# A linear-attention kernel with channel mix: whole 128-token chunks per head pair, casting loads with a DMA transpose, the max folded in by matmul, two-bank exponentials

One core of one Trainium2 chip. The metric is the device time of one execution in microseconds (us); lower is better. The kernel before takes 571.4 us (median of 4 runs in the comparison).

## The reference, cut to what matters

```python
def _attn_ref(q, k, v, w_phi):                       # 8 batches, 8 heads, 576 tokens, 64 wide; w_phi 64 x 128
    def phi(x):
        proj = np.einsum('bhsd,df->bhsf', x, w_phi)
        proj = proj - np.max(np.abs(proj), axis=-1, keepdims=True)
        return np.concatenate([np.exp(proj), np.exp(-proj)], axis=-1)
    q_p, k_p = (phi(q), phi(k))
    kv = np.einsum('bhsf,bhsd->bhfd', k_p, v)
    z = np.sum(k_p, axis=2)
    num = np.einsum('bhsf,bhfd->bhsd', q_p, kv)
    den = np.einsum('bhsf,bhf->bhs', q_p, z)[..., None] + 1e-06
    return num / den

def _moe_ref(x, mu_k, mu_r, w_k, w_v, w_r):          # x: 8 x 576 x 512, from the attention
    x_prev = # x one token later, zero first
    xk = mu_k * x + (1.0 - mu_k) * x_prev
    xr = mu_r * x + (1.0 - mu_r) * x_prev
    k = np.maximum(xk @ w_k, 0.0)                    # 512 -> 1024
    v = k * k @ w_v                                  # 1024 -> 512
    r = 1.0 / (1.0 + np.exp(-(xr @ w_r)))
    return r * v
```

The second part is called MoE below, as the code does, and its first three lines the mix. The work comes in 32 units, one for each pair of heads of a batch ("a pair"), four pairs a batch; after a batch's four pairs its mix and MoE follow, and these overlap with the next batch's pairs.

## The kernel before: the parts that the change touches

```python
def attention_pair(b, hp):
    for hh in range(2):                                   # 12 plain fp32 loads a pair, all from SP
        nc.sync.dma_start(out=q_nat[:, 0:NC4, 64*hh:64*hh+64], in_=q[b, h, 0:NC4*128, :]. ...)
        # ... q tail, k, k tail, v, v tail
    for (nat, T) in ((q_nat, qT), (k_nat, kT)):           # fp32 transposes on PE, evicted on DVE
        for ci in range(NC4):
            nc.tensor.matmul(ps_t[:, ci, :], lhsT=nat[:, ci, :], rhs=ident_f32, is_transpose=True, ...)
        # ... the tail chunk of 64 rows by itself
        nc.vector.tensor_copy(T[:, 0:NC4*128], ps_t...)
    # ... q and k projections, one bank at a time
    nc.vector.tensor_reduce(mk[:, 0:2, :], ps_pk, axis=AX.X, op=ALU.max, apply_absolute_value=True)
    nc.gpsimd.tensor_tensor(v1, vv, emki.to_broadcast(...), op=ALU.mult)     # exp(-max k) into v
    nc.gpsimd.tensor_tensor(v2, vv, emk.to_broadcast(...), op=ALU.mult)
    nc.scalar.activation(k_p[:, 0:2, :, :], ps_pk, AF.Exp)                   # 512 elements each
    # ...
    nc.scalar.activation(cq, mq, AF.Exp, scale=2.0)                          # max of q: a correction afterwards
    for hh in range(2):                                   # the heads one after the other
        # ... kv of this head (PSUM tag sm, one buffer), copy, nd1, nd2
        nc.vector.tensor_tensor(ndc, ps_nd2, cq..., op=ALU.mult)
        nc.vector.tensor_tensor(ndc, ndc, ps_nd1, op=ALU.add)
        nc.vector.reciprocal(rden, ndc[:, :, 64:65])
        nc.gpsimd.tensor_tensor(x_sc[...], ndc[:, :, 0:64], rden..., op=ALU.mult)
    # ... five transposes of x, copy to xT on ACT
```

## Time and profile before

| | before |
|---|---|
| time, median | 571.4 us (570.7 to 573.4, 4 runs) |
| span of the profiled run, mean granted TensorE clock | 571.3 us, 0.82 |
| busy: PE, DVE, ACT, POOL | 75%, 58%, 49%, 45% |
| pairs: first xT copy, mean distance, from the last one to the end | 37.3, 16.0, 37.7 us |
| DMA packets | 125,343 |

PE is the engine that multiplies matrices, DVE the vector engine, ACT the scalar engine, POOL is GpSimd, and SP issues DMAs. No engine is full. The reading that matters is the last line but one: 32 pairs follow each other at 16 us, so a pair's chain of waits sets the time, and what a change is worth shows in the distance between equal instructions of neighbouring pairs. The lines that carry this are in the prediction.

### The profile page before, as it was taken

The page shows a single profiled execution, that of the slowest core. Times are in us where ns is not written, and L with a number is a line of the kernel's source. Part 1 is how long each engine was busy: PE and PEld are TensorE (multiplying, and loading weights), DVE is VectorE, ACT ScalarE, POOL GpSimd, SP SyncE. Part 2 cuts the span into 40 slices and gives each one's busy share as a digit, 9 for nine tenths or more (in the row PEclk, how much of TensorE's full clock was granted, in tenths as well). Part 3 has the DMA queues.
Part 4 walks back from the last instruction along what each step waited for, and adds up shares of the span by engine and source line. Part 5 has one row for each costly group of instructions (what it writes and reads, how often), then busy time and mean ns, then how long its engine had stood idle before and what let it go on. Part 6 is the DMA issues. An engine that isn't in the chain of part 4 may idle for free. (4 is left out here: it accounts for less than half of the span.)

```text
span 571.3 us, 9500 instructions
## 1 busy us (share of the span) xinstructions
PE 428.0 (75%) x3200; PEld 259.8 (45%) x3200; DVE 330.9 (58%) x691; ACT 280.4 (49%) x780; POOL 255.7 (45%) x575
## 2 busy tenths in 40 slices
PE   0366655779787896779787896779787896779797
PEld 0144443555355443555355543555355444555352
DVE  0255458556865569556875469555775469555802
ACT  3553443565536544565436544565436553665141
POOL 2022334663346533663356433663256533663170
PEclk9995565789958897789968796789968796788979
DMA  7864222223322243223322233223312243001102
GB/s 198 251 151 106 64 57 47 63 63 100 89 46 53 61 126 73 63 62 98 87 46 64 61 118 71 64 63 89 99 39 56 63 117 84 0 2 38 46 1 83
DMA packets 125343, 43.68 MB, mean 76 GB/s; under 512 B 118512, under 2 KB 118640, under 8 KB 125296
## 3 DMA queue, kind: packets, MB, share of 16 engines
q1 hardware_dynamic: 125296, 43.09, 29.6%
q8 instruction: 25, 0.41, 0.3%
q14 instruction: 22, 0.18, 0.1%
HBM read 33.62 MB, written 9.44 MB: 75 GB/s over the span
## 5 line engine op out<-in xcount | busy, mean ns | idle before, releaser
L284 PE MATMUL ps_k<-xk,wk_bf 128*128 128x288 bf16 x512 | 115.4, 349 | 9.9 <-DVE xk L270 6.6
L288 POOL TENSOR_TENSOR kk<-krelu 128x288 bf16<-128x288 bf16 x128 | 86.4, 684 | 76.3 <-ACT krelu L287 67.8
L194 POOL TENSOR_TENSOR v<-v_nat,emk 128x650 bf16<-128x650 f32 x32 | 41.3, 1290 | 122.8 <-ACT emk L190 116.0
L251 POOL TENSOR_TENSOR x_sc<-ndc,rden 128x320 bf16<-128x320 f32 x64 | 49.9, 780 | 86.2 <-DVE rden L250 80.9
L287 ACT ACTIVATE krelu<-ps_k 128x288 bf16<-128x288 f32 x128 | 52.1, 417 | 67.0 <-PE ps_k L284 54.2
L302 PE MATMUL ps_v<-wv_bf,kk 128*128 128x512 bf16 x320 | 84.7, 381 | 0.0
L284 PEld LDWEIGHTS <-wk_bf 128*128 128x128 bf16 x512 | 56.9, 117 | 42.4 <-issue 25.5
L160 ACT ACTIVATE q_pT<-ps_pq 128x512 bf16<-128x512 f32 x64 | 38.6, 604 | 43.4 <-PE ps_pq L156 43.4
L246 DVE TENSOR_TENSOR ndc<-ps_nd,cq 128x325 f32<-128x325 f32 x64 | 31.9, 498 | 45.6 <-PE ps_nd L242 23.2
L228 PE MATMUL ps_kv<-v,k_p 128*128 128x65 bf16 x320 | 25.1, 222 | 40.7 <-POOL v L193 38.2
L228 PEld LDWEIGHTS <-k_p 128*128 128x128 bf16 x320 | 22.4, 114 | 72.4 <-issue 57.2
L134 DVE CAST qT<-ps_t 128x512 bf16<-128x512 f32 x32 | 22.1, 690 | 54.3 <-PE ps_t L129 54.3
L299 ACT ACTIVATE rt<-ps_r 128x512 bf16<-128x512 f32 x40 | 23.9, 597 | 55.9 <-PE ps_r L296 55.0
L296 PE MATMUL ps_r<-wr_bf,xr 128*128 128x512 bf16 x160 | 50.5, 412 | 0.0
L305 DVE SCALAR_TENSOR_TENSOR ob<-rt,ps_v 128x512 f32<-128x512 bf16 x40 | 27.3, 683 | 36.2 <-ACT xT L260 14.4
L234 DVE CAST kv_sb<-ps_kv 128x130 bf16<-128x130 f32 x64 | 18.8, 293 | 50.2 <-PE ps_kv L231 49.3
L161 ACT ACTIVATE q_pT<-ps_pq 128x64 bf16<-128x64 f32 x64 | 14.2, 222 | 66.6 <-PE ps_pq L157 66.6
L193 POOL TENSOR_TENSOR v<-v_nat,emki 128x650 bf16<-128x650 f32 x32 | 44.4, 1386 | 0.0
L302 PEld LDWEIGHTS <-kk 128*128 128x128 bf16 x320 | 29.3, 98 | 29.5 <-issue 9.4
L162 ACT ACTIVATE q_nT<-ps_pq 128x512 bf16<-128x512 f32 x64 | 38.4, 601 | 0.0
L238 PE MATMUL ps_nd<-kv_sb,q_pT 128*128 128x65 bf16 x320 | 25.8, 224 | 15.3 <-DVE kv_sb L234 15.3
L238 PEld LDWEIGHTS <-q_pT 128*128 128x128 bf16 x320 | 24.1, 120 | 27.5 <-issue 22.4
(81 smaller groups left out, 908.3 us busy)
## 6 DMA issues: line engine op xcount, KB each, us to landing
q_nat<-in_q_dram SPq DMA_DIRECT2D x64, 128.0 KB, 2.4
k_nat<-in_k_dram SPq DMA_DIRECT2D x64, 128.0 KB, 2.4
v_nat<-in_v_dram SPq DMA_DIRECT2D x64, 128.0 KB, 2.4
out_dram<-ob SPq DMA_DIRECT2D x32, 256.0 KB, 2.0
wstage<-in_moe_w_k_dram SPq DMA_DIRECT2D x1, 2048.0 KB, 8.3
wstage<-in_moe_w_v_dram SPq DMA_DIRECT2D x1, 2048.0 KB, 8.5
q_nat<-in_q_dram SPq DMA_DIRECT2D x64, 16.0 KB, 2.3
k_nat<-in_k_dram SPq DMA_DIRECT2D x64, 16.0 KB, 2.2
```

Of the source, the lines that this page charges most:

```text
L160: nc.scalar.activation(qp[:, 0:512], ps_pq, AF.Exp)
L162: nc.scalar.activation(qn[:, 0:512], ps_pq, AF.Exp, scale=-1.0)
L193: nc.gpsimd.tensor_tensor(v1, vv, emki.to_broadcast([128, NC, 2, 65]), op=ALU.mult)
L194: nc.gpsimd.tensor_tensor(v2, vv, emk.to_broadcast([128, NC, 2, 65]), op=ALU.mult)
L228: nc.tensor.matmul(ps_kv[:, 0:65], lhsT=k_p[:, ci, hh, :], rhs=v1[:, ci, hh, :], start=(ci == 0), stop=False)
L238: nc.tensor.matmul(ps_nd1[:, ci, :], lhsT=q_pT[hh][:, ci * 128:(ci + 1) * 128], rhs=kv_sb[:, 0:65], start=(ci == 0), stop=(ci == NC - 1))
L251: nc.gpsimd.tensor_tensor(x_sc[:, :, 64 * hh:64 * hh + 64], ndc[:, :, 0:64], rden.to_broadcast([128, NC, 64]), op=ALU.mult)
L284: nc.tensor.matmul(ps_k[:, 0:sw], lhsT=wk_bf[:, c, fc * 128:(fc + 1) * 128], rhs=xk[:, c, s0:s0 + sw], start=(c == 0), stop=(c == NDC - 1))
L287: nc.scalar.activation(krelu, ps_k[:, 0:sw], AF.Relu)
L288: nc.gpsimd.tensor_tensor(kk[:, fc, s0:s0 + sw], krelu, krelu, op=ALU.mult)
L296: nc.tensor.matmul(ps_r, lhsT=xr[:, c, cs:cs + 128], rhs=wr_bf[:, c, :], start=(c == 0), stop=(c == NDC - 1))
L302: nc.tensor.matmul(ps_v, lhsT=kk[:, fc, cs:cs + 128], rhs=wv_bf[:, fc, :], start=(fc == 0), stop=(fc == NFC - 1))
```

## The change

The intent: both heads of a pair go through one round instead of two, without a correction pass afterwards. Token p*4+j of a head stands in chunk j, row p, so that a load moves 1 KB a row; the 64-token tails of two heads share a chunk, which makes 9 full chunks. q and k are cast to bf16 by the load and transposed by one DMA per batch. The max of q is subtracted in PSUM: it is split into a high and a low bf16 part (`mhl`), transposed, and added to the projection by matmuls with a selector. Exponentials read two PSUM banks (1024 elements) at once. The tail rounds of two batches' MoE are joined.

Names used below: `v12` is v scaled by exp(-max k) and by exp(max k), in two POOL multiplies; `mT` is the transposed max of q, and the selectors are the matmuls that add it; `kv` is the product of k's exponentials with v12, `nd` holds numerator and denominator, `x_sc` is their quotient, and `xs` is its transpose, which the mix reads after a shift copy on POOL. The tails are the last 64 tokens of a head. A FIFO is an engine's queue, which it works off in order.

```diff
+            for (src, base) in ((k, 16), (q, 0)):
+                nc.gpsimd.dma_start(                                   # fp32 -> bf16
+                    out=flat[:, (base + 4 * a0) * 128:(base + 4 * a1) * 128]...,
+                    in_=src[b, hs, 0:SM, :].rearrange("h (p j) d -> p h (j d)", j=4))
+            # ... tails; v on SP
+            for (g0, g1) in rng:
+                nc.sync.dma_start_transpose(out=flatT[:, g0:g1, :], in_=flat[:, g0 * 128:g1 * 128])
...
+        ps_k = psum.tile([128, 8, 128], FP, name="ps_k", tag="P", bufs=2)       # two banks
+        ps_t = psum.tile([128, 4, 128], FP, name="ps_t", tag="B", bufs=2)       # tails; later mT
+        nc.vector.tensor_reduce(mk[:, :, 0:4], ps_k..., op=ALU.max, apply_absolute_value=True)
+        nc.vector.tensor_reduce(nm[:, 8:9], ps_t[:, 0, :], ..., negate=True)
+        nc.scalar.activation(em[:, 0, :], mkf, AF.Exp, scale=-1.0)
+        for pn in range(2):
+            nc.gpsimd.tensor_tensor(v12[:, pn, :, 0:64], vp..., em[:, pn, :]..., op=ALU.mult)
+        nc.scalar.activation(k_p, ps_k, AF.Exp)
+        nc.scalar.activation(k_n, ps_k, AF.Exp, scale=-1.0)
+        ps_q = psum.tile([128, 8, 128], FP, name="ps_q", tag="P", bufs=2)
+        nc.vector.tensor_reduce(nm[:, 0:8], ps_q, ..., negate=True)
+        nc.gpsimd.tensor_copy(mhl[:, 0:9], nm)
+        nc.gpsimd.tensor_tensor(mhl[:, 9:18], nm, mhl[:, 0:9], op=ALU.subtract)
+        nc.tensor.transpose(ps_mT, mhl, ident)
+        nc.vector.tensor_copy(mT, ps_mT)
+        ps_qT = psum.tile([128, 2, 4, 128], FP, name="ps_qT", tag="P", bufs=2)
+            nc.tensor.matmul(ps_qT[:, par, :, :]..., lhsT=wph[:, par, :], rhs=qkT[...], start=True, stop=False)
+                nc.tensor.matmul(ps_qT[:, par, g, :], lhsT=sel[:, 2 * g + par, :], rhs=mT, ...)
+        # t_p, t_n, q_p, q_n; kv (tag B) of both heads; kv copy; nd in two halves (tag B):
+            nc.vector.reciprocal(rden, ps_nd[:, :, 64])
+            nc.vector.tensor_tensor(x_sc[...], ps_nd[:, :, 0:64], rden..., op=ALU.mult)
+        # ps_x (tag B), copies to xs on DVE
...
     for b in range(B):
+        if b + 1 < B:
+            cur = load(b + 1, [(0, NP)])
         for hp in range(NP):
             attention_pair(...)
         if b >= 1:
             moe_batch(b - 1)
```

## The prediction

> **What bounds the kernel now.** I read the busy shares first, then the stretch before any MoE work (54 to 72 us) in order of time, then one tile's line for the pace.
>
> ```profile
> span 571.3 us, 9500 instructions
> PE 428.0 (75%) x3200; PEld 259.8 (45%) x3200; DVE 330.9 (58%) x691; ACT 280.4 (49%) x780; POOL 255.7 (45%) x575
> ```
>
> No engine is full. So the order of work, not an engine, sets the pace. The timeline from one k transpose's eviction to the next pair's shows it:
>
> ```profile
> 53.80 0.69 DVE L134 CAST kT<-ps_t 128x512 bf16<-128x512 f32 x1 [0.16 <-PE ps_t L129]
> ...
> 54.55 0.61 PE L175 MATMUL ps_pk<-wph,kT 128*128 128x256 bf16 x2
> ...
> 55.20 0.69 DVE L184 TENSOR_REDUCE mk<-ps_pk 128x4 f32<-128x512 f32 x1 [0.37 <-PE ps_pk L175]
> ...
> 56.99 0.21 ACT L191 ACTIVATE emki<-mk 128x10 f32<-128x10 f32 x1
> ...
> 57.18 1.27 POOL L194 TENSOR_TENSOR v<-v_nat,emk 128x650 bf16<-128x650 f32 x1 [5.56 <-ACT emk L190]
> ...
> 58.42 1.27 POOL L193 TENSOR_TENSOR v<-v_nat,emki 128x650 bf16<-128x650 f32 x1
> ...
> 59.74 0.43 PE L228 MATMUL ps_kv<-v,k_p 128*128 128x65 bf16 x5 [1.68 <-POOL v L193]
> ...
> 62.02 0.43 PE L228 MATMUL ps_kv<-v,k_p 128*128 128x65 bf16 x5 [0.43 <-ACT q_nT L163]
> ...
> 63.93 0.50 DVE L246 TENSOR_TENSOR ndc<-ps_nd,cq 128x325 f32<-128x325 f32 x1 [0.77 <-PE ps_nd L242]
> ...
> 65.58 0.72 POOL L251 TENSOR_TENSOR x_sc<-ndc,rden 128x320 bf16<-128x320 f32 x1 [1.62 <-DMA v_nat<-in_v_dram]
> ...
> 66.36 0.72 PE L256 MATMUL ps_x<-ident_bf,x_sc 128*128 128x128 bf16 x5
> ...
> 67.73 1.06 PE L129 MATMUL ps_t<-ident_f,k_nat 128*128 128x128 f32 x4
> ...
> 68.82 0.69 DVE L134 CAST kT<-ps_t 128x512 bf16<-128x512 f32 x1 [0.16 <-PE ps_t L129]
> ```
>
> The columns are start and duration in us. One head pair follows the next with hardly any overlap: 68.82 - 53.80 = 15.02 us. Two POOL multiplies, two kv/nd rounds in turn (one PSUM buffer, tag sm, passes from kv to the q tail and back), the POOL scaling, the x transposes and only then the next q/k transposes. Later, with MoE matmuls in the gaps, the big q projection of a first head comes at 301.18 and again at 315.54: 14.36 us. The MoE rides along for nothing.
>
> ```profile
> L258 ACT COPY xT<-ps_x x32: 585/587/590, 37.3 to 533.6; 128x512 bf16<-128x512 bf16 x32
> ```
>
> The xT copy ends each pair: (533.6 - 37.3)/31 = 16.0 us a pair on average, 37.3 us to the first, and 571.3 - 533.6 = 37.7 us for the last batch's MoE alone. This is the sum that I predict with: 37.3 + 31 x 16.0 + 37.7 = 571.
>
> **What the Trainium skill says.** (1) "ScalarE: Activation LUTs", What ACT_TABLE_LOAD costs: an activation with immediate scale takes 186 ns + 0.833 ns an element, and neighbours overlap by 93 ns. The trace agrees: 512 elements 604 ns (612 by it), 256 elements 393 to 406 (399). So 1024 elements in one instruction should take 1.04 us, against 2 x 0.60. (2) "DMA: Bandwidth & Descriptors", SWDGE vs HWDGE vs iDMA: a DMA that casts must be issued from GpSimd, whose cores write its descriptors; a transpose must come from SP or ACT. Before has neither (all loads are on SP's queue, 0.4 to 0.6 us of issue each), so no line shows what such an issue costs POOL. (3) "Advanced Engine Details and Errata", X-Bar Transpose (TRN2): 350 to 400 GB/s. A batch is 36 x 128 x 128 x 2 B = 1.18 MB, so 3.4 us, an estimate from that page; no run shows it yet. (4) "SBUF — State Buffer", Who interferes with whom: a DVE instruction with two SBUF inputs blocks against a POOL one that reads SBUF. It agrees: the xk mixes take 779 ns at least, 812 in the middle, up to 1478 beside POOL.
>
> **The change part by part, per pair unless said.**
>
> Transposes and loads. Gone: 10 fp32 transposes on PE, four evictions on DVE (2 x 0.69 + 2 x 0.22 = 1.8 us), six of the POOL memsets. In their place per batch 6 casting loads, 3 v loads and one DMA transpose, issued a whole batch ahead (two buffers), about 45 us before use. Bandwidth was 76 GB/s of the core and packets grow from 256 B to 1 KB, so they should hide.
>
> ACT. k and q exponentials: 4 x 1.04, tails 2 x 0.40, small 2 x 0.23: 5.4 us against 8.1 before (the xT copies of 0.81 move to DVE). With MoE (8 x 0.60 + 4.5 x 0.60, half of a tail round 1.1, over 4 pairs = 2.2): 7.6.
>
> DVE. Reduces of 1024 from PSUM at 1.07 ns an element (692 against 418 ns for 512 and 256): 2 x 1.24; tails 0.42 + 0.28; mT 0.22; kv 0.40; two of rden and multiply 2 x (0.18 + 0.48); xs copies 0.69 + 2 x 0.2. Sum 6.2, against 8.3. The cq correction (two passes over 325 a head) is gone. MoE: diff 1.4, mixes 8 x 0.73 + 8 x 0.15, outputs 4.5 x 0.68 = 11.5 a batch, 2.9 a pair. Together 9.1.
>
> POOL. v12 2 x 1.3, small ones about 0.5, squares (8 x 1.09 + 4 x 0.39)/4 = 2.6: 5.7, against 8. To this comes descriptor writing, for which I take 1 to 3 us an instruction: 1.5 to 4.5 a pair.
>
> PE, in columns: projections 9 x 256, max transpose 128, transposed q 2 x 512 + 8 x 128 + 2 x 128, kv and nd 1300 each, x 640: 7,976, against 8,232 (and the fp32 transposes took double). MoE, tails of two batches joined: 46,080 a batch against 49,152; 11,520 a pair. At 0.42 ns a column (four 512-column ps_r in 0.86 us at full clock): 8.2 us, at the granted 0.83: 9.9.
>
> So every engine fits in 10 us; now the chain. It runs through tag B (two buffers, five tiles a pair: ps_t, kv, nd, nd, x): the next ps_t needs the buffer of the last nd. From that release: ps_t 0.35, tail reduces 0.7, mhl on POOL 0.25, transpose 0.25, mT 0.25, selector matmuls and projection 1.0, exponentials 0.8 + 2.1 (beside them em 0.35 and v12 2.9 end at 4.2, before kv can start), last kv 0.4 (part hidden), kv copy 0.4, nd 0.8, rden and multiply twice 1.4. Sum 8.7. The k projection, its reduce and exponentials, and the q reduce (4.5 us of work) can be done in the pair before, as tag P frees in time. One round of kv/nd replaces two, and the POOL scaling and transposes have left the chain.
>
> DVE, PE and this chain are now close (9.1, 8.2 to 9.9, 8.7), so they collide: eight chain steps each find on DVE, ACT or POOL an instruction of 0.6 to 1.2 us under way about half of the time, 0.3 us each, 2.4. That gives **11.2 us a pair**.
>
> Start. 33 GpSimd DMAs (24 for the split first batch, 3 weights, 6 for the next) stand before the first v12 on POOL; at 1 us each, then some 9 us to the pair's end: 43 us. End: 6% fewer columns, but a tail round after: 38. Sum: 43 + 31 x 11.2 + 38 = **428 us**; I say 430.
>
> **Rivals.** (a) POOL becomes the bound: the big loads have 1024 rows each; if writing their descriptors takes 5 to 10 us, POOL is held some 25 us a batch, its FIFO stops v12 and the squares, and the start grows to 60 us or more: 13 us a pair, 470 to 510. For it: nothing measured; against it: POOL has the most slack. (b) The DMA transpose is slow, over the 45 us that the prefetch allows: then load, transpose and buffer release set the batch, 55 to 60 us: 500 to 560. Against it is the page's rate. (c) The chain overlaps worse than I think, since the scheduler puts v12 in front of mhl on POOL (adds 2.6 us) or queues the 1 us exponentials badly: 13.5 us a pair, 500. For it: before shows that orders once fixed are kept even where they idle (5.56 us on POOL). (d) All goes well, 9.7 us a pair, PE bound at nearly full clock: 380.
>
> **Range and chances.** Main line 430; (d) sets the low end at 385, (a) and (c) the high end at 500. Only (b) in its worst form, or a start and a POOL both far worse, reaches 560: 0.04 for slower, 0.04 for the same, 0.92 for faster.
>
> **What would show it.** The ps_x transposes should come every 11 us (right) or 13 and more (a or c). POOL idle before v12 waiting for em is the main line; POOL held by DMA issues is (a); PE waiting for a DMA of qkT after the first batch is (b); the mhl copies behind v12 are (c). ACT's busy time should fall to some 215 us, DVE's to 265, 1024-element exponentials to 1.04 us. DVE busy above 80% with PE's clock near 1 would mean an engine, not the chain, is the bound. The prediction falls if the first pair ends after 60 us or the pace is over 13.

## The result, and the profile after

| | before | after |
|---|---|---|
| time, median (range, 4 runs each) | 571.4 us (570.7 to 573.4) | 508.1 us (506.5 to 512.2) |
| ratio, 95% interval | | 0.889 (0.885 to 0.894) |
| granted TensorE clock of the profiled run | 0.82 | 0.94 |
| packets | 125,343 | 84,515 |

Every ratio here is from the fast runs of both kernels in the same rounds, so it is not quite the ratio of the medians quoted. The direction was right; 508 us is outside the range of 385 to 500.

First the busy line of the page, then the xs copies, which end each pair as the xT copies did before, and the kv copies, which I use as the beat below.

```profile
span 507.3 us, 7519 instructions
PE 336.2 (66%) x2832; PEld 194.5 (38%) x2832; DVE 296.2 (58%) x615; ACT 213.2 (42%) x389; POOL 247.1 (49%) x374
L267 DVE COPY xs<-ps_x x32: 409/418/425, 57.8 to 471.3; 128x512 bf16<-128x512 bf16 x32
L236 DVE CAST kv<-ps_kv x32: 413/429/430, 53.0 to 468.3; 128x260 bf16<-128x260 f32 x32
```

The sum that was predicted as 43 + 31 x 11.2 + 38 reads 57.8 + 31 x 13.34 + 36.0 = 507.3. The end is right; the start is 15 us too long and the pace, (471.3 - 57.8) / 31, costs 31 x 2.14 = 66 us. By place in the batch (batches 2 to 8), the mean distances of the kv copies are 15.9, 15.1, 11.3 and 9.9 us. The first pairs are the slow ones, and the last ones come close to the 8.7 us of the predicted chain. No engine is full: the busy shares of PE and ACT fell, DVE's stayed at 58%, and POOL's rose from 45% to 49%.

What PE waits for in front of the kv matmuls (group, with idle time and releasers last):

```profile
L231 PE MATMUL ps_kv<-v,k_p 128*128 128x65 bf16 x256 | 16.4, 209 | 58.4 <-POOL v L181 55.9 <-POOL mhl L197 2.5
```

55.9 us go to waiting for v12 on POOL. And the start, POOL in order of time:

```profile
32.72 0.20 POOL L197 CAST mhl<-nm 128x9 bf16<-128x9 f32 x1
44.87 0.93 POOL L118 DMA_DIRECT2D nat<-in_k_dram  x1 [11.95 <-DMA qkT<-nat]
45.82 2.49 POOL L178 TENSOR_TENSOR v<-vt,em 128x640 bf16<-128x640 f32 x2
48.25 0.27 POOL L181 CAST v<-em 128x20 bf16<-128x20 f32 x1
48.40 0.20 POOL L198 TENSOR_TENSOR mhl<-nm,mhl 128x9 bf16<-128x9 f32 x1
```

The issue of a load (0.93 us) stands in front of pair one's v12 and between the two steps of its max. It is the first load of the third batch, which cannot start before the first batch's DMA transposes free a nat buffer, so everything behind it on POOL stands still for 11.95 us. The same happens again at 62.55 us in front of the second pair.

### The profile page after: what moved, and what is told of

The parts are those of the page before. It is cut to its first block, busy times and chain, and to the rows that moved or that the text cites. A ratio compares the mean times of both kernels' runs of the same rounds, so it can differ in the third digit from the quotient of the medians.

```text
span 507.3 us, 7519 instructions
## 1 busy us (share of the span) xinstructions
PE 336.2 (66%) x2832; PEld 194.5 (38%) x2832; DVE 296.2 (58%) x615; ACT 213.2 (42%) x389; POOL 247.1 (49%) x374
## 2 busy tenths in 40 slices
DMA packets 84515, 40.92 MB, mean 81 GB/s; under 512 B 53120, under 2 KB 79360, under 8 KB 84480
## 4 chain that ended last, share of the span: by engine, by line
PE 31%; POOL 30%; DVE 18%; DMA 10%; issue 7%; ACT 4%; POOLq 0%; DVEq 0%; ACTq 0%
POOL v L178 15%; PE ps_v L319 6%; POOL kk L308 6%; DMA nat<-in_q_dram 5%; PE ps_h L304 5%; DMA qkT<-nat 4%; PE ps_kv L231 4%; PE ps_r L313 3%; DVE xr L290 3%; PE ps_nd L249 3%; DVE mk L161 2%; PE ps_k L153 2%; DVE tr L293 2%; POOL nat L124 2%; DVE x_sc L260 2%
## 5 line engine op out<-in xcount | busy, mean ns | idle before, releaser
L308 POOL TENSOR_TENSOR kk<-krelu 128x512 bf16<-128x512 bf16 (+1 forms) x96 | 85.1, 904 | 90.7 <-ACT krelu L307 90.2
L178 POOL TENSOR_TENSOR v<-vt,em 128x640 bf16<-128x640 f32 x64 | 82.6, 1314 | 1.1
L304 PE MATMUL ps_h<-xk,wk_bf 128*128 128x512 bf16 x256 | 77.2, 420 | 6.6 <-DVE xk L290 4.9
L307 ACT ACTIVATE krelu<-ps_h 128x512 bf16<-128x512 f32 (+1 forms) x96 | 46.2, 497 | 70.8 <-PE ps_h L304 61.6
L223 ACT ACTIVATE q_p<-ps_qT 128x1024 bf16<-128x1024 f32 x32 | 32.8, 1026 | 97.1 <-PE ps_qT L212 97.0
L185 ACT ACTIVATE k_p<-ps_k 128x1024 bf16<-128x1024 f32 x32 | 32.8, 1024 | 66.7 <-DVE mk L161 66.7
L231 PE MATMUL ps_kv<-v,k_p 128*128 128x65 bf16 x256 | 16.4, 209 | 58.4 <-POOL v L181 55.9
L161 DVE TENSOR_REDUCE mk<-ps_k 128x8 f32<-128x1024 f32 x32 | 39.1, 1221 | 24.6 <-PE ps_k L153 24.4
L194 DVE TENSOR_REDUCE nm<-ps_q 128x8 f32<-128x1024 f32 x32 | 39.0, 1218 | 14.2 <-PE ps_q L191 14.1
L207 PE MATMUL ps_qT<-qkT,wph 128*128 128x512 bf16 x64 | 29.3, 458 | 11.2 <-DVE nm L194 10.4
L319 PEld LDWEIGHTS <-kk 128*128 128x128 bf16 x288 | 26.4, 98 | 25.1 <-POOL kk L308 2.6
L290 DVE SCALAR_TENSOR_TENSOR xr<-diff,mu_r_t,xs 128x512 bf16<-128x512 bf16 x32 | 34.8, 1088 | 0.0
L224 ACT ACTIVATE q_n<-ps_qT 128x1024 bf16<-128x1024 f32 x32 | 33.4, 1044 | 0.0
```

What stands on the lines that cost most here:

```text
L161: nc.vector.tensor_reduce(mk[:, :, 0:4], ps_k.rearrange("p (h j) f -> p h j f", h=2), axis=AX.X, op=ALU.max, apply_absolute_value=True)
L178: nc.gpsimd.tensor_tensor(v12[:, pn, :, 0:64], vp.rearrange("p (s d) -> p s d", d=D), em[:, pn, :].to_broadcast([128, 10, D]), op=ALU.mult)
L194: nc.vector.tensor_reduce(nm[:, 0:8], ps_q, axis=AX.X, op=ALU.max, apply_absolute_value=True, negate=True)
L224: nc.scalar.activation(q_n, qT8, AF.Exp, scale=-1.0)
L231: nc.tensor.matmul(ps_kv[:, pn, h, :], lhsT=kx[:, c, :], rhs=v12[:, pn, 5 * h + j, :], start=(pn == 0 and c == 0), stop=False)
L290: nc.vector.scalar_tensor_tensor(out=xo[:, c, :], in0=diff[:, c, 0:SM], scalar=mu[:, c:c + 1], in1=xs[:, c, 0:512], op0=ALU.mult, op1=ALU.add)
```

## The experiments

18 kernels ran. All were compared with the kernel before on the same chip (its medians were 571.5 to 573.0 us). Where a result is wrong on purpose, the text says so; those five (e5, e6, e7, e9, e10) ran twice each, the others four or five times. An instruction's place in its engine's queue is fixed when the kernel is compiled: the compile-time scheduler takes the program's order as priority and its own simulated times. `tc.issue_after(x)` puts what stands in its block behind x on the same engine (in e1's trace no v12 multiply precedes the max subtraction any more; in the changed kernel's, 10 do).

### First four: was it the order on POOL, the loads, or the mix?

e1: v12 behind the max subtraction on POOL.

```diff
-        # emt and v12 multiplies ahead of the k exponentials
+        sub = nc.gpsimd.tensor_tensor(mhl[:, 9:18], nm, mhl[:, 0:9], op=ALU.subtract)
+        with tc.issue_after(sub.ins):
+            # emt and v12 multiplies
```

> The two v12 multiplies are queued on POOL behind the max subtraction of the same pair; nothing else changes. POOL-order theory: in 10 of 32 pairs of the changed kernel the multiplies (2.5 us) stand in front of the max copies, so the selector matmuls and the q exponentials wait 2.7 to 3.5 us longer; taking this away gives 25 to 35 us: about 478 us (470 to 490), and no pair with the subtraction after the multiplies. DVE-burst theory (the mixing of a batch in one go holds the slow pairs): within 1% of 508, because those pairs wait for DVE in any case.

Measured: 510.0 us (ratio 0.893), no gain. The first pairs of a batch still take 16.9 us. The issues of loads were left where they were, and POOL's wait for transposes in front of them rose from 25.0 to 30.4 us.

e2: the next batch's loads and the weights behind the first pair's v12.

```diff
             attention_pair(b, hp, qkT, vt)
+            if hp == 0:
+                with tc.issue_after(last_v12[0].ins):
+                    if b + 1 < B: cur = load(b + 1, [(0, NP)])
+                    if b == 0: load_weights()
```

> The loads of the next batch (and the weights) are queued on POOL behind the first pair's v12 instead of in front of it. Head-of-line theory: the first v12 starts near 27 us instead of 45.8, the first pair ends near 40 instead of 58 us, the second loses no 8 us either, and the whole gains 20 to 30 us: about 482 us. Rival (the DMA engines are full in the first 60 us, so the first batch's transposes and loads set the start in any case): first pair at 50 or later, gain under 8 us.

Measured: 488.3 us (0.853). The first kv copy comes at 30.9 us in place of 53.0, but the second one follows only 25.1 us later. DVE shows why:

```profile
41.06 0.22 DVE L203 COPY mT<-ps_t 128x128 bf16<-128x128 bf16 x1 [1.40 <-PE ps_t L201]
54.85 1.23 DVE L104 TENSOR_SCALAR wv_bf<-wv_bf 128x4096 bf16<-128x4096 bf16 x1 [13.56 <-DMA wv_bf<-in_moe_w_v_dram]
55.99 0.42 DVE L237 CAST kv<-ps_kv 128x260 bf16<-128x260 f32 x1
```

The halving of wv, which nobody needs yet, waits on DVE for its load, in front of the kv copy. The steady pace stays at 12.9 us over batches 2 to 8. So the gain is the start.

e3: the mix of each head pair right behind it instead of in one burst, with the shift copy of xs on POOL for each pair.

```diff
-    xk, xr = mix(b)                      # in one burst, after the next batch's pairs
+    attention_pair(b, hp, qkT, vt)
+    mix_pair(b, hp)                      # channel chunk hp only: shift copy (POOL), diff, xk, xr (DVE)
```

> The mixing of a batch's four column blocks (on DVE, about 13 us in one go after the batch) is done block by block right behind each head pair. DVE-burst theory: the first two pairs of a batch (16.6 and 14.2 us now, the last two 11.3 and 10.0) come down to about 12.5 each, and the time by 20 to 35 us: about 480 us; the last batch's end also shrinks by some 5 us. POOL-order theory: the first pairs stay slow because of the multiplies in front of the max copies and the loads; the gain is only the 5 us at the end, 500 us or more.

Measured: 592.2 us (1.036), much slower. POOL spent 200.9 us blocked on the shift copy that waits for the xs copy, in front of the next pair's v12. e4 was all three together:

> All three together. If the three losses are separate and the chain of 8.7 us plus collisions is the bound that is left, then 40 to the first pair, 31 x 11, and 33 at the end: about 415 to 435 us. If they are one loss seen from three sides, it stays near the best of the three single ones, 475 us or more.

Measured: 529.6 us (0.925). The shift copy's cost outweighs the rest. None of these shortened the pace by more than 0.2 us a pair (e3 and e4 raised it to 16.0 and 14.6), so my theory that GpSimd's queue or the mix burst sets it had no support left. It is not refuted for the mix: e3 spread the mix but added the waits on POOL, so it is no clean test.

### Four ablations: is it the MoE at all?

e5 leaves out mix and MoE between the pairs; e6 keeps the mix alone; e7 keeps the MoE alone, fed from fixed tiles; e8 is e1 and e2 together.

```diff
-        if b >= 1:
-            moe_batch(b - 1)
+        # e5: nothing      e6: mix(b - 1)      e7: moe_batch(b - 1) with xk, xr = fixed tiles
```

> The changed kernel without any mix or MoE work between the pairs (only the last batch's at the end, its rows stored for every batch: wrong result on purpose). Read from it: the intervals of the xs copies. Theory COLLISION (the pace is 13.3 us where the chain alone is 8.7 because the previous batch's mix and MoE stand in front of chain steps in the FIFOs): from batch 1 on every pair takes 8.5 to 10 us, the first of a batch too, 290 to 310 us from the first to the last xs copy. Rival BOUNDARY (attention itself is slow at a batch's start: loads on POOL that wait for transposes, buffers of nat/qkT): first pairs stay at 14 us or more, later ones at 9 to 10. Rival CHAIN (my chain was too short): all pairs stay over 11 us.

> As the run without MoE, but with the mix of the previous batch (GpSimd's shift copy, the DVE passes) in its place in the loop; MoE still only at the end (wrong result on purpose). Theory COLLISION by DVE: the mix is 11.5 us of DVE and a shift copy per batch, so the first two pairs of a batch gain 3 to 6 us together over the run without it; the mean pace rises by 1 to 2 us a pair. If the mix is not what hurts, it rises by under 0.5 us.

> The changed kernel with the MoE of each batch in place but fed from fixed tiles, no mix and no shift copy in the loop (wrong result on purpose). If PE/ACT/POOL work of the MoE is what collides: pace 12 us or more. If it is the mix: pace 9.5 to 10.5 us, 60 us or more off the time of the whole kernel.

> Both the v12 multiplies behind the max subtraction (alone without gain) and the loads of the next batch behind the first pair's v12 (alone 488 us). Theory ORDER ON POOL in its corrected form (both hold up the same chain step of the first pair, and taking away one lets the other take its place): 465 to 480 us, first pairs of a batch 14 to 16 us in place of 18. Rival (the order on POOL is worth nothing in steady state; what the second gained was the start alone): 484 to 495 us.

| | time | mean distance of kv copies, batches 2 to 8 | clock |
|---|---|---|---|
| after | 508.1 | 13.1 | 0.94 |
| e5, no mix, no MoE | 546.4 | 13.9 (14.1 to 14.6 nearly everywhere) | 0.63 |
| e6, mix alone | 514.4 | 12.6 | 0.68 |
| e7, MoE alone | 434.7 | 11.7 | 0.94 |
| e8, e1 and e2 | 490.2 | 13.0 | 0.89 |

The collision theory falls: take all the MoE away and the pairs get longer, not shorter. The attention alone runs at 14.3 us a pair in every batch (the whole kernel's first batch, which has no MoE beside it, shows the same 14.1 and 14.3). With work beside them the pairs come out in other orders and are shorter: the later pair's q reduce, read below, stands in front of the mT copy in 29 of 32 pairs of e5, but in 17 of e6, 19 of e7 and 14 of the changed kernel. The test is not clean, then: taking work away also changed the order, and the clock. e7 lies between its two forecasts: with the MoE in place, leaving out the mix takes 13.1 to 11.7 us. (e7's time has no end of its own, as its MoE does not wait for the last pairs; its distances are what to compare.) e8 adds nothing to e2.

So the steady pair of e5 had to be read step by step. From one x_sc to the next pair's q projection:

```profile
306.10 0.49 DVE L260 TENSOR_TENSOR x_sc<-ps_nd,rden 128x320 bf16<-128x320 f32 x1
...
307.30 1.23 DVE L161 TENSOR_REDUCE mk<-ps_k 128x8 f32<-128x1024 f32 x1 [0.60 <-PE ps_k L153]
308.44 0.48 DVE L260 TENSOR_TENSOR x_sc<-ps_nd,rden 128x320 bf16<-128x320 f32 x1
...
309.27 0.42 PE L158 MATMUL ps_t<-wph,qkT 128*128 128x256 bf16 x1
...
309.51 0.42 DVE L267 COPY xs<-ps_x 128x512 bf16<-128x512 bf16 x1 [0.59 <-PE ps_x L265]
...
310.61 0.28 DVE L166 TENSOR_REDUCE nm<-ps_t 128x1 f32<-128x128 f32 x1
...
311.49 2.48 POOL L178 TENSOR_TENSOR v<-vt,em 128x640 bf16<-128x640 f32 x2
...
311.67 1.23 DVE L194 TENSOR_REDUCE nm<-ps_q 128x8 f32<-128x1024 f32 x1 [0.78 <-PE ps_q L191]
312.81 0.21 DVE L202 COPY mT<-ps_t 128x128 bf16<-128x128 bf16 x1
...
314.23 0.60 PE L231 MATMUL ps_kv<-v,k_p 128*128 128x65 bf16 x8 [2.35 <-POOL v L181]
...
314.63 0.62 PE L207 MATMUL ps_qT<-qkT,wph 128*128 128x512 bf16 x1
```

Five delays can be counted; the granted clock of this stretch is 0.50. A later pair's k reduce (1.23) stands between the two x_sc multiplies. The xs copies (0.42 and two small ones) stand in front of the tail reduces, about 0.6. A later pair's q reduce stands in front of the mT copy: the transpose ended at 311.88, so 0.93. The kv matmuls that wait for v12 stand on PE in front of the selector group, which could have begun at 313.0: 1.6. And PE at this clock takes 2.0 us for projection and selectors, where a pair of the changed kernel at full clock took 1.2 (297.68 to 298.84 us). Together 5.2 us, of which 4.4 are places in the queues and 0.8 is the clock, and 14.3 - 5.2 = 9.1.

### Four: the order forced

e9 forces two places, e10 two more, both without MoE. e11 is e10's order in the whole kernel, e12 adds e2's loads.

```diff
+        with tc.issue_after(last_sel.ins):        # kv matmuls behind the selectors (PE)
             nc.tensor.matmul(ps_kv[...], ...)
+        with behind(last_mT):                     # k reduce (e9: and q reduce) behind the mT of the pair before (DVE)
             nc.vector.tensor_reduce(mk[:, :, 0:4], ps_k...)
+        with behind(last_xsc):                    # e10: q reduce behind the second x_sc of the pair before
             nc.vector.tensor_reduce(nm[:, 0:8], ps_q...)
+        with tc.issue_after(tail.ins):            # e10: xs copies behind the next pair's tail reduces
             nc.vector.tensor_copy(xs[...], ps_x...)
```

> The run without MoE took 14.3 us a pair in every batch, so MoE work is not what makes pairs long. New theory ORDER: FIFO places that the compile-time scheduler chose put work of the next pair, or work that waits for v12, in front of this pair's chain. Read from its steady pair: kv matmuls that wait for v12 stand on PE in front of the selector matmuls (1.2 to 1.6 us), the next pair's q reduce stands on DVE in front of the mT copy (1.0), its k reduce between the two x_sc multiplies (1.2), the xs copies in front of the tail reduces (0.8). Here two places are forced: kv behind the selectors on PE, and k and q reduces of a pair behind the mT copy of the pair before on DVE (wrong result on purpose, as before). ORDER: 14.3 falls by 2.2 to 12.0 us (11.5 to 12.6). Rival CLOCK (PE at half clock when idle, that is what makes the chain long): stays over 13.5.

> In addition the q reduce is forced behind the second x_sc of the pair before, and the xs copies behind the next pair's tail reduces. ORDER: another 1.2 + 0.8 less some 0.5 that the q reduce still costs the tail reduces: 10.5 us a pair (10 to 11). CLOCK: over 13 us.

> The same forced order in the whole changed kernel with MoE (correct result). ORDER: pairs three and four of a batch stay at 9.5 to 10.5 us, the first two fall from 17 and 14 to some 14 and 12 as mix work still stands between chain steps; 465 to 485 us in place of 508. If the pairs of the whole kernel are long for another reason (mix, loads), 500 to 515 us.

> The forced order and the next batch's loads and the weights behind the first pair's v12 (which alone made 488). If the two add up: 445 to 465 us. If the order gains nothing in the whole kernel: 484 to 492.

Measured without MoE: e5 546.4, e9 466.5, e10 414.0 us; a steady pair 14.3, 11.2 to 12.1, and 8.3 to 9.3. The clock was 0.63, 0.67 and 0.79: it rose as the waits went, so the 0.8 us of low clock went in part with them (in the stretch below it is 1.00 at the selectors and 0.50 from kv on). One pair in four of e10 in batches two to five, the one beside the loads, still takes 14.2 to 14.6: at 185 us POOL shows five issues of loads (the first after 4.07 us of waiting for a transpose) in front of its first max step, and a sixth and both v12 multiplies between the two steps. The same stretch of e10:

```profile
216.33 0.49 DVE L277 TENSOR_TENSOR x_sc<-ps_nd,rden 128x320 bf16<-128x320 f32 x1
216.74 1.21 DVE L210 TENSOR_REDUCE nm<-ps_q 128x8 f32<-128x1024 f32 x1
...
217.19 0.27 PE L168 MATMUL ps_t<-wph,qkT 128*128 128x256 bf16 x1
...
218.20 0.28 DVE L177 TENSOR_REDUCE nm<-ps_t 128x1 f32<-128x128 f32 x1
...
219.44 0.22 DVE L218 COPY mT<-ps_t 128x128 bf16<-128x128 bf16 x1 [0.34 <-PE ps_t L216]
...
219.72 0.82 PE L228 MATMUL ps_qT<-mT,sel 128*128 128x128 bf16 x8 [0.32 <-DVE mT L218]
...
221.81 0.60 PE L248 MATMUL ps_kv<-v,k_p 128*128 128x65 bf16 x8 [1.16 <-POOL v L196]
...
225.28 0.49 DVE L277 TENSOR_TENSOR x_sc<-ps_nd,rden 128x320 bf16<-128x320 f32 x1
```

225.28 - 216.33 = 8.95 us, close to the chain of 8.7 us of the prediction: all that still stands in front of a chain step is the q reduce, some 0.4 us, ahead of the tail reduces. The selectors follow mT at once, and kv waits for v12 behind them, beside the exponentials.

In the whole kernel e11 took 486.2 us (0.851): 22 us gained, 11 of them in the first batch. Over batches 2 to 8 the places read 17.5, 12.4, 10.8 and 9.6 (50.3 us a batch; after 52.2). With mix and MoE back, then, the forced order runs at 12.6 us a pair, where without them (e10) it ran at 9.7 over the same batches. e12 took 490.5: the two do not add up. In e12 the fourth pair comes 15 us earlier than in e11, though the second again comes 24 us after the first, held by the halving of wv; but the later batches run at 13.3 us a pair in place of 12.6.

### The last six: what holds the first pairs in the whole kernel

e13: e11 with the two max steps on DVE (the xs copies now stand behind the second of them). e14: the mix also held behind the first pair's mT. e15: also loads and weights behind the first v12, and the halving behind the fourth pair.

```diff
-        nc.gpsimd.tensor_copy(mhl[:, 0:9], nm)
-        nc.gpsimd.tensor_tensor(mhl[:, 9:18], nm, mhl[:, 0:9], op=ALU.subtract)
+        nc.vector.tensor_copy(mhl[:, 0:9], nm)                                   # e13
+        nc.vector.tensor_tensor(mhl[:, 9:18], nm, mhl[:, 0:9], op=ALU.subtract)
+        with tc.issue_after(first_mT[b + 1].ins): xk, xr = mix(b)                # e14
+        # e15: load(), load_weights() as in e2; the halving behind the fourth pair's mT
```

> The forced order, and the two small max subtraction steps on VectorE in place of GpSimd, which takes GpSimd out of the max chain (correct result). If GpSimd's queue is what holds the first pairs of a batch (v12, squares and load issues in front of the subtraction, 3 to 5 us): first pairs fall from 16 to 19 us to 13 or 14, the start by some 10 us, as pair one's and two's subtraction no longer waits behind blocked loads (though v12 still does, so perhaps not): 445 to 465 us. If not: 480 to 490.

> In addition the mix of the batch before is held on VectorE behind the first pair's mT copy (correct result). If the mix, which waits for GpSimd's shift copy, in front of mT is what holds the first pair: another 2 to 4 us a batch, 15 to 30 us less than the run before. If it is not: within 5 us of it.

> In addition the loads of the next batch and the weights behind the first pair's v12, and the halving of wv behind the fourth pair's mT copy (correct result). In the earlier runs with loads behind, the second pair came 24 us after the first, as the halving stood on VectorE waiting for its load (13.6 us idle) in front of the kv copy. Expected: first xs copy at 35 us, second 10 to 14 us later; 25 to 35 us less than the run before, 400 to 425 us. If the start is bound by the DMA instead (full for the first 62 us), the four first pairs still end at 85 to 95 us and it gains under 10.

Measured: 479.4, 477.2 and 465.5 us (0.837, 0.833, 0.812). The max on DVE is worth some 7 us; the first pairs stay at 17.7 us, so POOL's part in the max chain is not what holds them. Holding the mix gains nothing that the intervals separate. In e15 the fourth pair's kv copy comes at 64.3 us in place of 89.0 (e14), but only 11.6 us reach the end: the later batches got slower, 12.9 against 12.4 us a pair, so the 400 to 425 us were missed. Why is not tested. The loads' issues now stand behind the first v12 and in front of POOL's shift copy, for which the mix waits. And 28 of the 64 max steps on DVE took 0.42 to 1.23 us where the others took 0.17 to 0.26, each ending within 0.04 us of the end of a POOL instruction; over batches 2 to 8 they cost 25.4 us more than 0.18 us each would, 12.1 in e14 (13 such steps). That difference is as large as the slowdown, 28 x 0.5 us. PE in e15 at the border of two batches:

```profile
267.84 0.22 PE L274 MATMUL ps_nd<-kv,t_n 128*128 128x130 bf16 x1
...
269.94 1.89 PE L341 MATMUL ps_v<-wv_bf,kk 128*128 128x512 bf16 x8
271.67 1.03 PE L335 MATMUL ps_r<-wr_bf,xr 128*128 128x512 bf16 x4
272.66 1.89 PE L341 MATMUL ps_v<-wv_bf,kk 128*128 128x512 bf16 x8
...
274.61 0.60 PE L164 MATMUL ps_k<-wph,qkT 128*128 128x256 bf16 x4
```

The last nd of a batch ends at 268, and the next batch's first k projection comes at 274.6, behind a block of MoE matmuls: in the program, `moe_batch(b - 1)` comes before the next batch's pairs and so has priority. e16 moves the MoE of a batch behind the first pair of the batch after next; e17 spreads it in blocks of four between the pairs and takes the mix behind the first pair; e18 is e16's move in the changed kernel with no other edit.

```diff
             attention_pair(b, hp, qkT, vt)
+            if hp == 0 and b >= 2:
+                moe_batch(b - 2)                 # mix(b - 1) stays behind the four pairs of b
```

> As the run with all (465.5), but the MoE of a batch is emitted behind the first pair of the batch after next, so that pair has priority over it (correct result). If PE's block of ps_r and ps_v in front of the first k projection is what holds the first pair: it falls from 18.5 to 13 us or less, 6 x 5 = 30 us less, 430 to 445 us. If that MoE block is only moved to the second pair: 460 to 468.

> As the run with all, but the mix stands behind the batch's first pair and the MoE's blocks are spread in the program, four behind each of the three other pairs (correct result). If it is a matter of evenness: all pairs 10.5 to 12 us, 36 + 31 x 11.2 + 36 = 420 us. If PE or DVE with 77% and 72% of busy time are already near what such chains allow: 445 to 465.

> The changed kernel with one edit: the MoE of a batch is emitted behind the first pair of the batch after next, the mix stays where it was (correct result). If the priority of the MoE over the next batch's first pair is a cause by itself: 470 to 490 us, first pairs of a batch down from 16.6 to 12 or so. If it pays only with the forced order (the queue of v12, max and mix work holds the first pairs anyway): 500 to 515 us.

| | time | ratio to before | places 1 to 4 of a batch, mean us (kv copies) |
|---|---|---|---|
| after | 508.1 | 0.889 | 15.9, 15.1, 11.3, 9.9 |
| e15 | 465.5 | 0.812 | 17.7, 12.3, 11.4, 10.0 |
| e16 | 432.9 (3 fast runs of 5) | 0.755 (0.751 to 0.759) | 9.8, 16.0, 11.0, 11.1 |
| e17 | 458.1 | 0.801 | 10.3, 19.2, 9.6, 11.6 |
| e18 | 492.5 | 0.860 | 12.2, 14.9, 11.1, 11.6 |

e16 is correct and beats both kernels: 139 us less than before, some 75 less than after (in other rounds). Its only profile fell in a slow run (span 438.8), so its distances may be about 2% long (440.6 us against 432.9). The first pairs fell to 9.8 us; the long place moved on to the second pair but is shorter, so the theory that the block would only move is half right. e18 shows that the move alone, in the changed kernel, is worth about 16 us, just short of the 470 to 490 us; on top of the forced order and the earlier start it is worth 33. The second pair of e16, DVE and POOL:

```profile
317.50 3.04 POOL L190 TENSOR_TENSOR v<-vt,em 128x640 bf16<-128x640 f32 x2
...
318.12 1.24 DVE L210 CAST mhl<-nm 128x9 bf16<-128x9 f32 x1
...
319.26 1.82 DVE L312 SCALAR_TENSOR_TENSOR xk<-diff,mu_k_t,xs 128x512 bf16<-128x512 bf16 x1
320.48 0.73 POOL L193 CAST v<-em 128x20 bf16<-128x20 f32 x1
321.00 0.16 DVE L211 TENSOR_TENSOR mhl<-nm,mhl 128x9 bf16<-128x9 f32 x1
```

A mix instruction of 1.82 us (its kind takes 0.70 to 0.75 elsewhere in this pair) stands between the two max steps. The first max step is itself held, 1.24 us for a copy of nine columns that takes 0.17 to 0.20 in most other pairs, and both long instructions run beside POOL's v12 work: the first v12 multiply ends at 319.32, the copy at 319.35. In e16 22 of the 64 max steps are long in this way, 0.6 us a pair on average and nearly all in the second and third pairs of a batch. By these times, moving the max to DVE did not take POOL out of the chain; no run separates this. That the rest of the long place is the mix is read from this stretch, not shown: e17, which also moved the mix, only moved the long pair.

## Why the prediction was wrong, point by point

**The chain of 8.7 us was right as a sum.** e10's free pairs take 8.3 to 9.3 us, after's fastest pairs under 10. Single terms were off in both directions: in the stretch of e10 above the max steps took 0.7 us from the tail reduce to the transpose (0.25 said), and q's exponentials 2.5 (2.9 said). ACT's busy time (213 us, 215 said), the 1024-element exponentials (1.02 to 1.04 us) and the end (36, 38 said) were right too. DVE came out at 296 us, not 265, partly in mixes that ran beside POOL (the xr mix has a mean of 1.09 us and a minimum of 0.71).

**The step that failed is the collision term: "eight chain steps each find on DVE, ACT or POOL an instruction of 0.6 to 1.2 us under way about half of the time, 0.3 us each, 2.4".** (8.7 + 2.4 is 11.1; I wrote 11.2.) In the whole kernel the mean excess over the chain is 13.3 - 8.7 = 4.6 us, which leaves the pace 2.1 us a pair over the 11.2 predicted, or 66 us in all. The term treats meetings as chance and as short. The runs show two things in its place.

First, fixed places in the queues. In 29 of 32 pairs of e5 the same work stands in front of the same chain steps and costs 4.4 us without any MoE; forcing four places took the pair from 14.3 to 8.95 us, with the help of the clock. But e5's places are not the whole kernel's. In the trace of after a later k reduce stands between the two x_sc multiplies in 10 of 32 pairs, a q reduce in front of mT in 14, kv in front of the selectors in 13; only the xs copies stand in front of the tail reduces everywhere. So forcing the order there returns some 0.5 us a pair over batches 2 to 8 and 11 us in the first batch.

Second, the work of the batch before, in few and long pieces. With the order forced, mix and MoE add 2.9 us a pair (e10 9.7, e11 12.6), most of it in one place: the first pair takes 8.9 us in e10 and 17.5 in e11. The MoE's place in the program is one part of it: moving it took 0.9 us a pair off (e16 against e15). What is left in e16, 12.0 us a pair, stands mostly in the second pair of each batch and is not settled; nor is how the 4.6 us of the unchanged order divide.

**The start failed in its mechanism.** "33 GpSimd DMAs at 1 us each, then some 9 us" gave 43; the issues cost 0.5 to 1.0 us each, and with some waits between them the 33 were done at 32.6 us, as said, by luck. But a 34th stood in front of v12, a load of the third batch, and waited 11.95 us for transposes to free its buffer, at the head of POOL's queue. With the loads behind v12 and the halving out of the way (e15) the first kv copy came at 32.0 us in place of 50.9 and the fourth at 64.3 in place of 89.0 (e14, the same kernel without these two).

**The rivals.** (c) named the right thing, bad orders at 13.5 us and 500, and (a) the right start, 57.8 against "60 us or more", though not by its mechanism. I took them for alternatives when I drew the range; both numbers came true at once, (a)'s by luck. (c)'s example, v12 in front of the max, is true of 10 of 32 pairs but worth nothing by itself (e1). (b) failed: the transposes are slower than assumed, but after the first batch they cost almost nothing in waits.

## What to carry to other kernels

When a change shortens a chain to what fits beside other work, its gain depends on where each instruction stands in its engine's queue: read one pair in order of time, list what stands in front of each chain step, and force those places. Read it in the kernel that counts: taking all the other work away looks like a quick test of a collision theory, but here it also changed the order and the clock, and the places that it showed were worth 5 us a pair there and 0.5 us in the whole kernel. A load that needs a buffer and a conversion of weights that have not arrived held an in-order queue for 11.95 and 13.56 us, though they ran for 0.93 and 1.23; bulk work that stands earlier in the program stood 6.5 us in front of the next batch's first step. And where a short step of the chain takes several times its usual length, see what ran beside it.

## What the Trainium skill lacked or had wrong

- "Advanced Engine Details and Errata", X-Bar Transpose (TRN2): it expects 350 to 400 GB/s. Here the six whole-batch transposes (36 x 128 x 128 bf16, 1.18 MB) landed 8.0, 9.2 and 9.9 us (min, median, max) after the start of their issue, and the issue alone took 6.4 to 7.3 us on SP: 1.18 MB / 9.2 us = 128 GB/s from issue to landing. The packets of 256 B in that time, theirs but for some 512 rows of v, took 5.4 to 6.5 us from the first to the last, which makes 180 to 220 GB/s. Loads of v and stores ran beside them, so this is no rate of a transpose alone.
- "DMA: Bandwidth & Descriptors", SWDGE vs HWDGE vs iDMA: the section has no figure for what an issue costs GpSimd's own queue. Here the issue of a casting load of 1024 rows held POOL for 0.89 to 0.97 us, one of 256 rows for 0.62 to 0.84 and one of 64 rows for 0.52 to 0.62 (in the trace of after); an issue whose buffer was not free held it for 11.95 us.
- None of the pages named here says how much the order that the compile-time scheduler chooses can matter: the same instructions without MoE took 14.3 us a pair in one order and 8.95 in another (546.4 and 414.0 us in all, with the granted clock at 0.63 and 0.79).
